# One order table drawn anew, first scores split and narrowed, counts' check and taps moved back, values of two groups in whole rows

## The chip, the cores and the metric

The kernel runs on one core of a Trainium2 chip. The metric is the device time of one execution in microseconds (us); less is better. Three executions of the kernel before took 346.62, 346.76 and 347.51 us, median 346.76. A fourth, profiled one took 346.18 us; the trace and all rows below are of that one.

## What is computed

Three stages follow each other on a batch of 2 sequences of 768 positions: banded attention (each query sees the 96 positions up to itself and the first 8 positions of the sequence), then a gated feed-forward with a convolution of three taps along the sequence, then a gated unit that mixes positions with a 768x768 matrix.

```python
def _attn_ref(q, k, v, n_global, n_local):
    scores = scale * np.matmul(q, k.transpose(0, 1, 3, 2))
    keep = is_global | is_local
    bias = -slopes[:, None, None] * dist[None, :, :]
    scores = np.where(keep, scores + bias, -1e9)
    a = np.exp(scores - np.max(scores, axis=-1, keepdims=True))
    a = a / (np.sum(a, axis=-1, keepdims=True) + 1e-09)
    return np.matmul(a, v)
...
def _moe_ref(x, w_in, conv_w, w_out):
    h = np.maximum(x @ w_in, 0.0)
    hp = np.concatenate([zeros, h, zeros], axis=1)
    for k in range(K):
        conv_out += conv_w[k][None, None, :] * hp[:, k:k + S, :]
    gate = 1.0 / (1.0 + np.exp(-conv_out))
    return (h * gate) @ w_out
...
def _moe2_ref(x, w_in, w_spatial, b_spatial, w_out):
    h = np.maximum(x @ w_in, 0.0)
    u, v = (h[..., :d_ff // 2], h[..., d_ff // 2:])
    v_n = (v - mu) / np.sqrt(var + 1e-06)
    v_s = np.einsum('ts,bsd->btd', w_spatial, v_n) + b_spatial[None, :, None]
    return (u * v_s) @ w_out
```

## The kernel before

**Pieces.** The attention is cut into 6 groups of 256 queries (3 per sequence; `g` counts them), and each group into 4 pairs of heads. A group and a pair make a unit `u` (24 in all): two tiles of 128 queries (`t` = 0, 1) for two heads. A unit's steps are: its q and k are loaded (`qk_load`, tile `qk`, three buffers); TensorE makes the scores (`scores`, L789: 128 queries against 256 keys for each tile and head, the two heads in the two halves of the rows); VectorE adds the bias and takes the minimum of the negated row (`soften`, L808, tile `sb`); ScalarE takes the exponential (L826); the result is transposed, for groups 0 and 1 (`PLAINS`) on TensorE in fp32 (`turn_p`, L839) and for the others by a transposing DMA; TensorE multiplies it with the values (`weigh`, L894, or L900 to L902 for the other groups); VectorE divides (L906 to L911); TensorE turns the output (L942) into the tile `x`.

In group 0 the first tile of queries has only 160 keys that can matter, and L808 reads 160 columns there, while L789 computes 256 for every tile. Groups 0 to 2 (`NATS`) use one fp32 product (4 matmul instructions to a unit, 8 records in the trace); groups 3 to 5 use three products of split operands (12 instructions).

**Values.** `v_load` loads the values of a group into the one tile `v`. For groups 0 and 1 each pair of heads occupies 130 columns (`VW`): a column of ones, 128 values, a column of ones. The ones are set once by a memset on GpSimd (L732) ahead of the first load, and each load writes the 128 columns between them in pieces of 512 bytes.

**Setup.** At the start the two counts (`n_global`, `n_local`) arrive as words; VectorE casts them (`word`, L567), TensorE spreads them over the partitions (L570), VectorE builds the masks and the first two biases (L573 to L594). `flags` (in `setup_rest`, L625 and L635 to L637) tests the counts against what the banded way can do; the answer is read at the end of the kernel. The taps of the convolution are loaded as `craw` and decoded (L655 to L670).

**Weights.** Weights arrive as 8-byte floats in tiles `raw` (512 KB each) and are decoded on GpSimd (L659), ScalarE (L655) and VectorE (L665, L670) and split in two fp16 halves. The feed-forward's matmuls are L1017 (`inner`) and L1087 (`outer`), the third stage's L1171, L1294, L1382 and L1444.

**What sets the order.** Every step is a task of a planner (`Plan`), and the table `ORDER` names for each step in turn its task number, its engine and, where it opens one, its PSUM bank. The instructions of each engine are then issued in exactly that order. While replaying the table the planner keeps a clock of its own from assumed costs. It uses this clock for one thing that reaches the chip: where TensorE's next step would start later than the one before ends, `emit` fills the gap with matmuls whose result nobody reads (`warm`, L988, on the tile `hl`; called fillers below), as many as this formula gives:

```python
share, each = (0.95, 0.213) if start < COLD_TO else (0.8, 0.107)
for _ in range(int(share * (start - busy) / each)):
    warm()
```

Every DMA of the kernel but one is issued by SyncE (SP) in the table's order; a load whose buffer is still in use holds those behind it.

## Time and profile before

| what | value |
|---|---|
| median of three executions | 346.76 us (346.62 to 347.51) |
| the profiled execution | 346.18 us |
| its span, first to last instruction | 344.4 us |
| TensorE busy | 336.9 us (98%) |
| VectorE, ScalarE, GpSimd busy | 305.3, 244.0, 140.6 us |
| moved by DMA | 43.62 MB |

The span is 1.8 us shorter than the profiled execution. A busy TensorE is not a TensorE at work on the result: the fillers count as busy. So the profile has to be read by stretches, and in the first 60 us by what each matmul is.

### The profile page before, as it was taken

The numbers are of one execution on the slowest core, as the hardware profiler recorded it, in microseconds if no ns is written. First come the engines' busy times: TensorE is split into PE (matmuls) and PEld (weight loads), VectorE is DVE, ScalarE is ACT, GpSimd is POOL, SyncE is SP. The second block draws the span as 40 slices with busy tenths as digits, with TensorE's granted clock in tenths as the row PEclk, the third lists the DMA queues.
The fourth block names the chain that finished last, engine by engine and source line by source line (L and its number), as shares of the span: only waits on it lengthen the run. The fifth ranks groups of instructions, "written<-read, shape, count | busy, mean of one in ns | idle before, by whom it ended". The sixth has DMA issues, their size and how long they took to land.

```text
span 344.4 us, 7937 instructions
## 1 busy us (share of the span) xinstructions
PE 336.9 (98%) x2824; PEld 246.5 (72%) x2824; DVE 305.3 (89%) x892; ACT 244.0 (71%) x619; POOL 140.6 (41%) x233
## 2 busy tenths in 40 slices
PE   8999999999999999999999999999999999999993
PEld 5888779898888888888996757755556666654451
DVE  6999999999999999999988899999998999999400
ACT  4999999999999999999865552776555233334331
POOL 5747698599757877737451000000124012010000
PEclk9999999999999999999999999999999999999998
DMA  7999638799659984645770000001461000000332
GB/s 246 349 386 300 214 105 302 175 209 256 125 149 205 278 173 79 184 79 109 102 221 0 2 1 0 2 1 48 126 206 52 0 2 0 3 30 0 124 124 101
DMA packets 46115, 43.62 MB, mean 127 GB/s; under 512 B 34674, under 2 KB 36466, under 8 KB 45554
## 3 DMA queue, kind: packets, MB, share of 16 engines
q1 hardware_dynamic: 46064, 43.02, 45.7%
q8 instruction: 24, 0.39, 0.5%
q14 instruction: 25, 0.20, 0.2%
q10 hardware_dynamic: 2, 0.00, 0.0%
HBM read 31.48 MB, written 3.15 MB: 101 GB/s over the span
## 4 chain that ended last, share of the span: by engine, by line
PE 96%; DMA 1%; DVE 0%; ACT 0%; issue 0%; DVEq 0%
PE bank L1017 19%; PE bank L1087 18%; PE bank L1294 12%; PE bank L1444 9%; PE bank L1382 9%; PE bank L1171 9%; PE bank L789 7%; PE bank L894 4%; PE bank L839 2%; PE bank L988 2%; PE bank L942 2%; DMA qk_dt_float<-in_qk 1%; PE bank L900 1%; PE bank L901 1%; PE bank L902 1%; ACT wk_dt_float L454 0%
## 5 line engine op out<-in xcount | busy, mean ns | idle before, releaser
L1017 PE MATMUL bank<-x_dt_float,w1h_dt_float 128*128 128x260 f16 (+1 forms) x384 | 65.5, 273 | 0.0
L1087 PE MATMUL bank<-hh_dt_float,w2h_dt_float 128*128 128x256 f16 (+2 forms) x192 | 52.4, 273 | 0.0
L1017 PE MATMUL bank<-x_dt_float,w1l_dt_float 128*128 128x260 f16 (+1 forms) x192 | 52.4, 273 | 0.0
L1087 PE MATMUL bank<-hl_dt_float,w2h_dt_float 128*128 128x256 f16 (+2 forms) x192 | 52.3, 272 | 0.0
L1087 PE MATMUL bank<-hh_dt_float,w2l_dt_float 128*128 128x256 f16 (+2 forms) x192 | 52.3, 272 | 0.0
L1030 DVE SCALAR_TENSOR_TENSOR bank<-hp_dt_float,cwt,bank 128x254 f32<-128x254 f32 (+2 forms) x96 | 46.1, 486 | 3.3 <-ACT bank L1024 0.6
L470 POOL TENSOR_TENSOR ph_dt_float<-sb_dt_float,ph_dt_float 128x512 f16<-128x512 f32 x29 | 34.2, 1184 | 20.5 <-ACT ph_dt_float L456 12.4
L1017 PEld LDWEIGHTS <-w1h_dt_float 128*128 128x128 f16 x384 | 37.1, 97 | 5.7
L1087 PEld LDWEIGHTS <-w2h_dt_float 128*128 128x128 f16 x384 | 36.3, 98 | 5.4 <-issue 0.3
L808 DVE CUSTOM_DVE_ANT_0 sb_dt_float<-bank,bias_dt_float 128x256 f32<-128x256 f32 (+1 forms) x96 | 35.4, 402 | 1.6 <-PE bank L789 1.3
L1382 PE MATMUL bank<-ys_dt_float,w3uh_dt_float 128*128 128x384 f16 x128 | 31.2, 326 | 0.0
L826 ACT ACTIVATE sb_dt_float<-sb_dt_float,nb_dt_float 128x256 f32<-128x256 f32 (+1 forms) x64 | 29.6, 491 | 0.0
L659 POOL TENSOR_SCALAR raw_dt_float<-raw_dt_float 128x512 int32<-128x512 uint8 x28 | 19.0, 680 | 24.7 <-DMA raw_dt_float<-in_w 22.0
L1444 PE MATMUL bank<-w4h_dt_float,g_dt_float 128*128 128x512 f16 (+1 forms) x104 | 28.8, 363 | 0.0
L1171 PE MATMUL bank<-w3vh_dt_float,ys_dt_float 128*128 128x512 f16 x96 | 28.5, 379 | 0.0
L470 POOL TENSOR_TENSOR hl_dt_float<-ac_dt_float,hh_dt_float 128x254 f16<-128x254 f32 (+2 forms) x35 | 23.4, 678 | 10.7 <-DVE hh_dt_float L460 8.0
L1444 PEld LDWEIGHTS <-g_dt_float 128*128 128x128 f16 x156 | 15.2, 98 | 15.4
L1171 PEld LDWEIGHTS <-ys_dt_float 128*128 128x128 f16 x144 | 14.1, 98 | 15.3
L1294 PE MATMUL bank<-ws_dt_float,vn_dt_float 128*128 128x384 f16 x144 | 25.0, 326 | 0.0
L1050 ACT ACTIVATE bank<-bank 128x254 f32<-128x254 f32 (+2 forms) x48 | 16.9, 364 | 10.5 <-DVE bank L1030 10.2
L1024 ACT ACTIVATE bank<-hp_dt_float,cwt 128x254 f32<-128x254 f32 (+2 forms) x44 | 21.0, 477 | 0.5
L1055 DVE SCALAR_TENSOR_TENSOR ac_dt_float<-bank,hp_dt_float 128x254 f32<-128x254 f32 (+2 forms) x48 | 19.5, 418 | 2.0 <-ACT bank L1050 1.5
(198 smaller groups left out, 907.6 us busy)
## 6 DMA issues: line engine op xcount, KB each, us to landing
raw_dt_float<-in_w SPq DMA_DIRECT2D x20, 512.0 KB, 6.3
qk_dt_float<-in_qk SPq DMA_DIRECT2D x24, 336.0 KB, 4.6
v_dt_float<-in_vb SPq DMA_DIRECT2D x4, 1024.0 KB, 5.7
out_x<-wk_dt_float SPq DMA_DIRECT2D x11, 256.0 KB, 2.0
raw_dt_float<-in_wst SPq DMA_DIRECT2D x6, 384.0 KB, 3.8
raw_dt_float<-in_w3v SPq DMA_DIRECT2D x4, 512.0 KB, 5.5
raw_dt_float<-in_w3u SPq DMA_DIRECT2D x4, 512.0 KB, 4.4
v_dt_float<-in_vb SPq DMA_DIRECT2D x2, 768.0 KB, 5.1
```

Source lines behind the costliest of these rows:

```text
L470: self.engines[e].tensor_tensor(out=out, in0=in0, in1=in1, op=ALU.subtract)
L789: nc.tensor.matmul(self.ps(sp[h])[:, 256 * t : 256 * (t + 1)], x[r, t * P : (t + 1) * P], y[r, k0[t] : k0[t] + 256], start=n == 0, stop=n ...
L808: nc.vector.tensor_tensor_reduce(out=sb[:, h, :n], in0=self.ps(self.sp[u][h])[:, 256 * t : 256 * t + n], in1=self.m("bias", 2 * p + h)[:, ...
L826: nc.scalar.activation(out=sb[:, h, :n], in_=sb[:, h, :n], func=AF.Exp, scale=-1.0, bias=nb[:, h : h + 1])
L1017: nc.tensor.matmul(self.ps(acc)[:, :nx], w[f][:, k * P : (k + 1) * P], x[:, k, x0:], start=k == n == 0, stop=k == 3 and n == 2,)
L1024: nc.scalar.activation(out=ac(), in_=near(1), func=AF.Copy, scale=tap(1))
L1030: nc.vector.scalar_tensor_tensor(out=ac(), in0=near(j), scalar=tap(j), in1=ac(), op0=ALU.mult, op1=ALU.add)
L1087: nc.tensor.matmul(ps(), w[2 * d + k // 4][:, k % 4 * P : (k % 4 + 1) * P], x, start=k == n == 0, stop=k == 7 and n == 2,)
L1171: nc.tensor.matmul(ps(), x[:, y, k, tk], w[k], start=n == 0, stop=n == 11)
L1294: self.nc.tensor.matmul(self.ps(acc)[:, :HS], v[:, k, x, ek], w[:, k, y], start=n == 0, stop=n == 8)
L1382: nc.tensor.matmul(ps(), w[e4][:, k * P : (k + 1) * P], x[:, y, k, s], start=n == 0, stop=n == 11)
L1444: nc.tensor.matmul(ps(), x[:, y, k, tk], w[k][:, at], start=n == 0, stop=n == 11)
```

## The change

**Scores.** In group 0 the first tile's scores are computed for 160 columns instead of 256 (units 0 to 3, 8 matmuls in all). For units 0 and 1 (`SINGLE`) the two tiles become two steps of the plan, so that VectorE's L808 of the first tile waits for the first two matmuls of the unit alone.

**Counts and taps.** The test of the counts gets a begin of 60 in the planner's time, and the taps' load one of 3.0.

**Values.** For groups 0 and 1 the host lays out an array `vp` in which every pair of heads has its 130 columns, so that a load writes whole rows (6,240 bytes for group 0, 8,320 for group 1). The memset of ones now follows each of these loads, since the load overwrites the columns.

**Planner.** It assumes the first transfer at 2.6 instead of 3.2 and the counts' word at 2.62 instead of 3.1. The table `ORDER` is another from its first line to its last. The program has 65 fillers instead of 60, and as many other matmuls as before.

The diff, of the table one line:

```diff
@@ -47,6 +47,8 @@
 
 BIASES = 2
 
+SINGLE = 2
+
 
 
 HALF = dict(w=8, x=9, h=12, y=12, g=12, v=8, s=16)
@@ -112,61 +114,61 @@
 SIGNS = "ABCDEFGHIJKLMNOPQRSTUVWXYZabcdefghijklmnopqrstuvwxyz0123456789-_"
 
 ORDER = (
-    "CHSAAGAWSDnGAnSAXGABDACGAZSADDAuSAbGAgSAEDBHGCMDAFPAGDCJA0CIGAHDAaP12AJDAKAASAAIDAMAAoGAdDBaSApA3AyDAYSANGAcDAOA",
...
+    "DqGAWSACGAoSAAGAZSA6SAcGABDAvSAEDADDAFPAXSAhSAGDAHDAaP01AMAAIDAbPAKAAJDAqA2AdDApGAeDAQAA0DBdSA5PANGAOAA1DA4P34Ag",
...
 )
 
 
@@ -179,7 +181,7 @@
     ENGINES = ("PE", "DVE", "ACT", "POOL", "SP")
     AFTER = dict(PE=0.21, DVE=0.13, ACT=0.14, POOL=0.1, SP=0.03)
     ISSUE, FLIGHT, LANDING, RATE = 0.45, 0.7, 0.9, 0.41e6
-    BEGIN, FIRST, TURN = 0.75, 3.2, 2.0
+    BEGIN, FIRST, TURN = 0.75, 2.6, 2.0
 
     def __init__(self, tc, room):
         self.tc, self.room = tc, room
@@ -333,9 +335,9 @@
 
 
 class Kernel:
-    def __init__(self, ctx, tc, vb, qk, qf, kf, vf, nw, w1, cw, w2, w3u, w3v, wst, bsp, w4, out):
+    def __init__(self, ctx, tc, vb, vp, qk, qf, kf, vf, nw, w1, cw, w2, w3u, w3v, wst, bsp, w4, out):
         self.tc, self.nc = tc, tc.nc
-        self.vb, self.qk, self.qf, self.kf, self.vf = vb, qk, qf, kf, vf
+        self.vb, self.vp, self.qk, self.qf, self.kf, self.vf = vb, vp, qk, qf, kf, vf
         self.nw, self.w1, self.cw, self.w2 = nw, w1, cw, w2
         self.w3u, self.w3v, self.wst, self.bsp, self.w4, self.out = w3u, w3v, wst, bsp, w4, out
         nc = tc.nc
@@ -508,11 +510,11 @@
 
         self.plan.add(dict(DVE=6.0), judge, reads=[acc, ("flag", 0)], writes=[("junk", 0)])
 
-    def load(self, out, in_, writes, size, reads=()):
+    def load(self, out, in_, writes, size, reads=(), begin=0.0):
 
         self.plan.add(
             dict(SP=Plan.ISSUE), lambda e: self.nc.sync.dma_start(out=out, in_=in_), reads=reads, writes=writes,
-            load=0.05 + size / Plan.RATE,
+            load=0.05 + size / Plan.RATE, begin=begin,
         )
 
     def parts(self, n, hi, lo, src, reads, wh, wl, scale=1.0):
@@ -585,7 +587,7 @@
             nc.vector.tensor_copy(out=rel[:, 256:288], in_=nl.to_broadcast([P, G]))
 
         add(dict(DVE=0.55), far, reads=[("rel", 0)], writes=[("keep", 0)], both=True)
-        add(dict(DVE=0.17), word, writes=[("word", 0)], begin=3.1)
+        add(dict(DVE=0.17), word, writes=[("word", 0)], begin=2.62)
         add(dict(PE=0.25), spread, reads=[("word", 0)], writes=[("words", 1)])
         add(dict(DVE=0.15), words, reads=[("words", 1)], writes=[("words", 0)])
         add(dict(DVE=1.1), masks, reads=[("words", 0)], writes=[("rel", 0), ("keep", 0)], both=True)
@@ -613,7 +615,7 @@
 
         self.load(
             self.craw.rearrange("p n t -> p (n t)").bitcast(I64), self.cw.rearrange("p f j -> p (f j)"),
-            [("craw", 0)], 24576,
+            [("craw", 0)], 24576, begin=3.0,
         )
         self.decode(self.cwt.rearrange("p f j -> p (f j)"), self.craw, [("craw", 0)], [("cwt", 0)])
 
@@ -626,7 +628,7 @@
                     out=self.within[:1, j : j + 1], in0=x[:1], scalar1=at, scalar2=None, op0=op
                 )
 
-        add(dict(DVE=1.0), flags, reads=[("word", 0)], writes=[("flag", 0)], both=True)
+        add(dict(DVE=1.0), flags, reads=[("word", 0)], writes=[("flag", 0)], both=True, begin=60.0)
 
     def counts(self, n):
         nc = self.nc
@@ -715,13 +717,10 @@
         b, c = divmod(g, NCH)
         n = 3 if c == 0 else 4
         if g in PLAINS:
-            v = self.m("v").rearrange("p (n d) -> p n d", d=VW)
-            if g == 0:
-                self.ones_beside(v, ("v", g, "one"))
-            self.load(
-                v[:, : n * NPAIR, 1 : 1 + 2 * D], self.vb[b, c, :, :n].rearrange("p a (n d) -> p (a n) d", d=2 * D),
-                [("v", g, "v")], n * P * 2048, [("v", g, "one")],
-            )
+            size = n * NPAIR * VW
+            v = self.m("v")[:, :size]
+            self.load(v, self.vp[g, :, :size], [("v", g)], 4 * P * size)
+            self.ones_beside(v.rearrange("p (n d) -> p n d", d=VW), ("v", g, "one"))
             return
         v = self.m("v")[:, :2048].rearrange("p (a n) -> p a n", a=4)[:, :n]
         self.load(v, self.vb[b, c, :, :n], [("v", g)], n * P * 2048)
@@ -780,18 +779,27 @@
             pairs = [(hi, hi), (lo, hi), (hi, lo)]
             cost, reads = 0.96, [("qk", u), ("qh", u)]
         sp = self.sp[u] = [self.plan.next("ps") for _ in range(2)]
-
-        def products(e):
-            for t in range(2):
+        short = i == 0 and g in NATS
+        less = 0.16 if short else 0.0
+
+        def products(ts):
+            for t in ts:
                 for n, (x, y) in enumerate(pairs):
                     for h in range(2):
-                        r = slice(64 * h, 64 * h + 64)
+                        r, cols = slice(64 * h, 64 * h + 64), 160 if short and t == 0 else 256
                         nc.tensor.matmul(
-                            self.ps(sp[h])[:, 256 * t : 256 * (t + 1)], x[r, t * P : (t + 1) * P],
-                            y[r, k0[t] : k0[t] + 256], start=n == 0, stop=n == len(pairs) - 1,
+                            self.ps(sp[h])[:, 256 * t : 256 * t + cols], x[r, t * P : (t + 1) * P],
+                            y[r, k0[t] : k0[t] + cols], start=n == 0, stop=n == len(pairs) - 1,
                         )
 
-        self.plan.add(dict(PE=cost), products, reads=reads, writes=sp, half=True)
+        if u >= SINGLE:
+            self.plan.add(dict(PE=cost - less), lambda e: products(range(2)), reads=reads, writes=sp, half=True)
+            return
+        for t in range(2):
+            self.plan.add(
+                dict(PE=0.5 * (cost + 0.283) - less * (t == 0)), lambda e, t=t: products([t]), reads=reads,
+                writes=[(*x, t) for x in sp], half=True,
+            )
 
     def soften(self, s):
         nc, add = self.nc, self.plan.add
@@ -810,7 +818,7 @@
                     scale=-0.125, scalar=3.0e38, op0=ALU.add, op1=ALU.min, accum_out=nm[:, h : h + 1],
                 )
             add(
-                dict(DVE=0.08 + 0.00105 * n), lowest, reads=[self.sp[u][h], ("bias", 2 * p + h)],
+                dict(DVE=0.08 + 0.00105 * n), lowest, reads=[(*self.sp[u][h], t), ("bias", 2 * p + h)],
                 writes=[("sb", s, h), ("nm", s, h)],
             )
         if g in PLAINS:
@@ -1687,10 +1695,12 @@
         near = [np.concatenate([vt[:, k - BACK : k], vt[:, :G]], axis=1) for k in (lo, lo + P) if k]
         rows += (near + near)[:2]
     vb = np.stack(rows, axis=1).reshape(B, NCH, 4, P, DM).transpose(0, 1, 3, 2, 4)
+    vp = vb.reshape(B * NCH, P, 4, NPAIR, 2 * D)[: len(PLAINS)]
+    vp = np.concatenate([vp[..., :1], vp, vp[..., -1:]], axis=-1).reshape(len(PLAINS), P, -1)
     vfull = vt.reshape(B, NT, P, DM).transpose(0, 2, 1, 3)
     w3 = moe2_w_in
     arrays = dict(
-        vb=vb, qk=qk, qf=qt, kf=kt, vf=vfull,
+        vb=vb, vp=vp, qk=qk, qf=qt, kf=kt, vf=vfull,
         nw=np.stack([np.asarray(n_global), np.asarray(n_local)]).astype(np.int64).view(np.uint16),
         w1=moe_w_in.reshape(4, P, 8, P).transpose(1, 2, 0, 3).reshape(P, 8, 512),
         cw=moe_conv_w.reshape(3, 8, P).transpose(2, 1, 0),
```

**TensorE, around the scores of unit 1.** Names: `qk` and `sb` with numbers are buffers, `ident` is the identity of a transposition. Lines L790, L847 and L996 of the changed kernel are L789, L839 and L988 of the one before. Before:

```order
L988 MATMUL bank<-hl_dt_float_76 128x256
L789 MATMUL bank<-qk_dt_float_122 128x256 x4
L839 MATMUL bank<-ident,sb_dt_float_123 128x128 x4
L789 MATMUL bank<-qk_dt_float_130 128x256 x4
L839 MATMUL bank<-ident,sb_dt_float_132 128x128 x4
L839 MATMUL bank<-ident,sb_dt_float_139 128x128 x4
L789 MATMUL bank<-qk_dt_float_88 128x256 x4
L839 MATMUL bank<-ident,sb_dt_float_123 128x128 x4
```

In the changed kernel, the same place:

```order
L996 MATMUL bank<-hl_dt_float_76 128x256
L790 MATMUL bank<-qk_dt_float_122 128x256 x2
L790 MATMUL bank<-qk_dt_float_122 128x160 x2
L847 MATMUL bank<-ident,sb_dt_float_123 128x128 x4
L996 LDWEIGHTS hl_dt_float_76
L996 MATMUL bank<-hl_dt_float_76 128x256
L847 MATMUL bank<-ident,sb_dt_float_132 128x128 x4
L790 MATMUL bank<-qk_dt_float_130 128x160 x2
L790 MATMUL bank<-qk_dt_float_130 128x256 x2
L847 MATMUL bank<-ident,sb_dt_float_139 128x128 x4
```

The two pieces of a unit stand next to each other, one of them is narrower, and a filler has come between two transpositions.

**TensorE, a unit of groups 3 to 5.** Before, each of the 12 stands between other matmuls, as here behind the products with the values:

```order
L902 MATMUL bank<-vh_dt_float_149,pt_dt_float_144 128x65
L789 MATMUL bank<-qh_dt_float32r 128x256 x2
L789 MATMUL bank<-qh_dt_float32r,qk_dt_float32r 128x256 x2
L789 MATMUL bank<-qk_dt_float32r,qh_dt_float32r 128x256 x2
L789 MATMUL bank<-qh_dt_float32r 128x256 x2
L789 MATMUL bank<-qh_dt_float32r,qk_dt_float32r 128x256 x2
L789 MATMUL bank<-qk_dt_float32r,qh_dt_float32r 128x256 x2
L1017 LDWEIGHTS w1h_dt_float_94
```

In the changed kernel, the end of the first of two places where the scores of two units follow each other:

```order
L790 MATMUL bank<-qh_dt_float32r,qk_dt_float32r 128x256 x2
L790 MATMUL bank<-qk_dt_float32r,qh_dt_float32r 128x256 x2
L790 MATMUL bank<-qh_dt_float32r 128x256 x2
L790 MATMUL bank<-qh_dt_float32r,qk_dt_float32r 128x256 x2
L790 MATMUL bank<-qk_dt_float32r,qh_dt_float32r 128x256 x2
L790 MATMUL bank<-qh_dt_float32r 128x256 x2
L790 MATMUL bank<-qh_dt_float32r,qk_dt_float32r 128x256 x2
L790 MATMUL bank<-qk_dt_float32r,qh_dt_float32r 128x256 x2
L1025 LDWEIGHTS w1h_dt_float_92
```

At these two places the second unit of a pair no longer stands between matmuls of another kind.

**GpSimd, the ones beside the values.** `v_dt_float_89` is the tile `v`; L661 is L659 before, L472 is L470, L731 is L732. Before, the one memset stands at the start:

```order
L549 IOTA keep_dt_float_80 128x32
L1039 MEMSET hp_dt_float_178 128x1
L732 MEMSET v_dt_float_89 128x16x2
masks.py:197 MEMSET ident 128x128
masks.py:199 AFFINE_SELECT ident<-ident 128x128
```

In the changed kernel, the second of two, with what stands ahead of it and behind it:

```order
L472 TENSOR_TENSOR w1l_dt_float_100<-wk_dt_float_136,w1h_dt_float_92 128x512
L661 TENSOR_SCALAR raw_dt_float_128<-raw_dt_float_128 128x512
L472 TENSOR_TENSOR w1l_dt_float_101<-wk_dt_float_138,w1h_dt_float_93 128x512
L472 TENSOR_TENSOR w1l_dt_float_102<-wk_dt_float_127,w1h_dt_float_94 128x512
L731 MEMSET v_dt_float_89 128x16x2
L661 TENSOR_SCALAR raw_dt_float_143<-raw_dt_float_143 128x512
L661 TENSOR_SCALAR raw_dt_float_137<-raw_dt_float_137 128x512
```

The memset now waits for a transfer, and the decoding of weights on GpSimd waits behind it.

## Rows read from the trace of the kernel before

**Rows 1.** The page: span; TensorE's busy tenths in 40 slices.

```profile
span 344.4 us, 7937 instructions
PE   8999999999999999999999999999999999999993
```

**Rows 2.** Windows: from:to, length, busy time (count) per engine, clock, DMA.

```profile
0.00:8.40 8.40, 6.96 (x33) 4.37 (x33) 5.47 (x29) 3.48 (x7) 4.58 (x21) 1.00 0.71 251
8.40:60.00 51.60, 51.25 (x431) 43.05 (x430) 49.39 (x164) 50.72 (x122) 37.15 (x58) 1.00 0.80 274
60.00:338.00 278.00, 278.00 (x2360) 198.97 (x2360) 250.44 (x703) 189.23 (x490) 98.85 (x156) 1.00 0.40 96
```

**Rows 3.** Windows of the fillers (L988) alone: TensorE, its weight loads, clock, DMA.

```profile
0.00:8.40 8.40, 4.49 (x23) 2.68 (x23) 1.00 0.71 251
8.40:60.00 51.60, 5.95 (x38) 3.47 (x37) 1.00 0.80 274
```

**Rows 4.** Timeline of the start: start, length, engine, line, operation, count, idle before.

```profile
1.19 2.10 PE L988 MATMUL bank<-hl_dt_float 128*128 128x256 f16 x9 [1.19 <-DVE hl_dt_float L538]
1.19 0.42 SPq L514 DMA_DIRECT2D qk_dt_float<-in_qk  x1
...
2.61 0.15 DVE L567 CAST word<-wt 1x8 f32<-1x8 uint16 x1
...
2.87 0.52 DVE L637 SCALAR_TENSOR_TENSOR cnt<-cnt,word 1x2 f32<-1x2 f32 x3
...
3.22 0.59 PE L570 MATMUL bank<-word,ones 1*128 1x8 f32 x2
...
4.07 1.44 PE L988 MATMUL bank<-hl_dt_float 128*128 128x256 f16 x6 [0.26 <-DVE wf L573]
...
5.42 0.83 DVE L594 SCALAR_TENSOR_TENSOR bias_dt_float<-rel_dt_float,keep_dt_float 128x288 f32<-128x288 f32 x2
...
5.43 2.08 PE L789 MATMUL bank<-qk_dt_float 64*128 64x256 f32 x8
...
7.44 1.05 PE L988 MATMUL bank<-hl_dt_float 128*128 128x256 f16 x8
...
7.56 0.33 DVE L808 CUSTOM_DVE_ANT_0 sb_dt_float<-bank,bias_dt_float 128x160 f32<-128x160 f32 x1 [1.31 <-PE bank L789]
...
8.42 1.13 PE L789 MATMUL bank<-qk_dt_float 64*128 64x256 f32 x8
...
9.49 0.66 PE L839 MATMUL bank<-ident,sb_dt_float 128*128 128x128 f32 x4
```

**Rows 5.** Timeline of TensorE, one unit of groups 3 to 5.

```profile
76.65 0.19 PE L902 MATMUL bank<-vh_dt_float,pt_dt_float 128*128 128x65 f16 x1
76.77 0.39 PE L789 MATMUL bank<-qh_dt_float32r 64*128 64x256 f32 x2
77.00 0.28 PE L789 MATMUL bank<-qh_dt_float32r,qk_dt_float32r 64*128 64x256 f32 x2
...
77.47 0.28 PE L789 MATMUL bank<-qk_dt_float32r,qh_dt_float32r 64*128 64x256 f32 x2
77.68 0.40 PE L1017 MATMUL bank<-x_dt_float,w1h_dt_float 128*128 128x260 f16 x2
```

**Rows 6.** Timeline of TensorE: values' products of unit 3, then of unit 4.

```profile
23.18 1.90 PE L894 MATMUL bank<-v_dt_float,pt_dt_float 128*128 128x65 f32 x16
...
33.12 1.11 PE L894 MATMUL bank<-v_dt_float,pt_dt_float 128*128 128x65 f32 x8
```

**Rows 7.** Timeline of SP: the load of group 1's values.

```profile
25.11 0.68 SPq L514 DMA_DIRECT2D v_dt_float<-in_vb  x1
```

**Rows 8.** Tile `v`: issue to landing of its loads, and its memset.

```profile
L732 POOL MEMSET v_dt_float<- x1: 142/142/142, 1.4 to 1.4; 128x32 f32 x1
...
DMA to landing us min/median/max: 5.0/5.5/6.5
```

**Rows 9.** Line L514, every load and store: issue to landing.

```profile
DMA to landing us min/median/max: 1.8/4.6/8.4
```

More of the change, by code (lines that the diff above doesn't have):

```diff
@@ new lines @@
+    "AArDALGAfACQSA2ABMDAyP5BBSD4GA7GAsDA3ABWSA8A6BLDARGBIP0BgDBOABkP12BhDBKGBNAAPGAzDBjABeP3BiAA9DBJABzP4AYGB3DB2DAU",
+    "AB6P0CUDCsGB5AB0DASAAjA5AiGA-DAtAB1GAkDAVGCXP24B8SB4ABPSCTDBfAATGAlDCRP6CVAEASCWADkP13CuDCKSCtDCSADDDDjSBCGDEDCv",
+    "ABsSCqP6CwAB7DEKGAuGBDA5BlSDBP2D0DEhSDFACxP4DzDDGABXGEFDCrAEEDBEDD1AB9GBYA3CYP0CyDDbP1EGACZABZDAmACaDD2AAnGBaDDH",
+    "P6DCADZP4DIDEHAECP0DcDCLGDaAEIP32BQGEDABFDBbADJDDdP4CDSCbAESP0EVDBcGCjSBRA1EUDDhP6EkDDeAElDCMA5BmGA_ADfDBSDEXAFN",
+    "GBAGEoP24EWAAwSDiDETABtGEmACNDBTDDlP6EiP0EnACODDmDBGACcSFaDFMSBuA3BHGDnDE-DBUAD3P5BvDEjABVGE9DB-A1FbDE7P0BnA6BwD",
@@ new lines @@
+    "DpP2D5AB_DE8ABoDFAAAxGCkGFBP3FdACADCEGD6ABpDDrADLSClA4D7DCzSFeP01DKAF5SE_AFCDC6SBxAFYP6CBAFvDByGEJP3FwDFZACmDDsA",
+    "CdGF8DBqADtDFzP0D8ABrGCFA6CnDFcADMGELAD9DDuAFtP4F9DFxACoDGAP51D-ACGDCpGDgAFyADvDCHDFuAF6P2EZGD_GF-AF0DFgP4DSSF_A",
+    "CCGFhAGMDGJP6F7AGLDEpP0GbDEMAFfGGNGGaDGKACIDGOAFiDGcGEqGGfP21GPAENDGdAErAGYDEyP6CeA5HbSGwDGZGEOAGWSGvDEsACfDGQP4",
+    "DoAGxGEPDC7GGeAG9DDwAG-DC0GGsACgDE0AEzGG0P2CJGGzAGRDC1A3EtDG_GDNA1DTGGBP5E1AC2DEBSEYP4ChAEQDEuADODERGGCAGyAC3DCi",
+    "GEaAHcAE2DHBADxGG1DEbAGtGG7AGDDHCP32HAAEvDE3ADPDG8GEwAHNAFkP5EcDITSC4AHOGGuSHRDDUA1HQDFDP0DQAHpDFlGC5GHqDEdADVDF",
@@ L170 @@
+    "DclAcqDblAcHDc2P3b7AcpDc5DcCAcmDcrP1cIAcyDcOAcNDc6DcUAcuP6b6DcsDc_DdqP7ctDcgDcBDcvDcZDdXP1caDdrAc7DcbAanDdsSaoDc",
+    "hAdwP6c1Dc8DcnAdMDdNDawDa9Dd2P7a-DdADdBDdODdCDdRP2d3Ac9Ad4SdFP7dSDdTDc0DdUAdeP0dEAdYDdlDdtP2dmDdnDdPDdoDdVDc3Ddz",
+    "P4duAdGDdxAdfDdySdgDdvSdZDdHDd-P5dIDdJDdDDdaDdbDeBP3dcDd_AdhDd0AeASdiDdKAd1SdQAeEP2d5P6eFAdWAeGSddAdjAeCAeQP0d6D",
+    "dpAd7Sd8P7eHP1eRDd9DeSSeDSeNP5eKP4eOAeIAePSeJSeLAeMS",
 )
```

94 lines of the change are left out of this document (40 added, 54 removed).

## Prediction

> **What bounds the kernel now.** I read the page first: TensorE's row is full from the second slice to the end of a span of 344.4 us [rows 1]. So the next view splits it. From 60 to 338 us TensorE is busy 278.00 of 278.00 us, and nothing that another engine does sooner can be seen there [rows 2]. In 8.4 to 60 us it is busy 51.25 of 51.60, but 5.95 us of that are 38 fillers (37 start in it), and before 8.4 us fillers make 4.49 us more [rows 3]. Fillers stand where the plan expects TensorE to wait, so some 10.4 us of fillers, 1.2 us ahead of the first one and the 0.35 us of idle time are all that a new order can win, besides making the work itself smaller. In 8.4 to 60 us ScalarE is busy 50.72 and VectorE 49.39 of 51.60 us [rows 2]: these two make the softmax and decode the weights there, and the fillers are what TensorE does meanwhile.
>
> The timeline of the start shows the chain: nine fillers, the spread of the counts at 3.22, six fillers, unit 0's scores at 5.43, eight fillers, unit 1's scores at 8.42 [rows 4]. VectorE has its two biases at 6.25 (5.42 and 0.83 on) and then stands 1.31 us until unit 0's scores end [rows 4].
>
> The granted clock reads 1.00 in all three stretches [rows 2], so its level at the start has to be taken from durations. Fillers of 256 columns follow each other at 0.226 us (1.19 to 3.22 in nine, 4.07 to 5.43 in six) until 7.44 and at 0.11 after it (7.44 to 8.42 in eight, less 0.1 for the change of kind that follows): 1.2 and 2.4 GHz. Before the rise TensorE had worked from 1.19 us on, with gaps of under 0.3 us [rows 4].
>
> A filler is an instruction, not a wait: it runs whether or not its wait would have come. TensorE's work in the new order can therefore be added up, and the end cannot come before it.
>
> **The change part by part, against the profiled execution (346.18 us, span 344.4; the median of the three others is 346.76, so I add the difference to the median).**
>
> *Start.* The order of the changed kernel has seven and five fillers where nine and six were, three fewer at 0.226 us: 0.68 us, and unit 0's scores could start at 4.75. The counts' word allows it: it is cast at 2.61 to 2.76 [rows 4], and the spread would start at 2.77. Removing the counts' test from VectorE's queue (0.52 us at 2.87 for its longest part, [rows 4]) gives nothing by itself, since VectorE waits for TensorE behind it; where it goes, after 60 us, VectorE has 27.6 us free [rows 2], so it costs nothing, and without that room about 0.9 us. The taps' load leaves the first place on SP, which brings unit 0's q and k (issued at 1.19, [rows 4]) forward by one issue, 0.42 us; when they land no row shows. If they land only just ahead of 5.43 now, the scores start at 5.0 and 0.25 us of the gain is lost.
>
> Unit 0 narrowed: a unit takes 1.07 us at full clock (8.42 to 9.49), 0.2 of it for the change of kind before and after, so four passes of 0.22; the first tile has two, and 96 of 256 columns less make 0.16 us, twice that at half clock: 0.32. Its scores then end at 6.44 instead of 7.44. Seven fillers follow instead of eight: if the clock rises where it rose, at 7.44, 4.4 of them run at 0.226 and 2.6 at 0.11, and unit 1 starts at 7.83 instead of 8.42: **-0.6 us**. This is the term that depends on the clock. If the rise came with the work, one us sooner, all seven fillers would run at 0.11, unit 1 would start at 7.3, and the term would be -1.1. The trace has one rise and cannot say which; I take -0.6, the smaller.
>
> The Trainium skill, page "TensorE: Matmul & The Clock Gate", Part 1, says that the warm-up is a budget of time and not a number of matmuls, and that the same kernel shows different numbers of slow matmuls from run to run. By that the term is -0.6 on average; this trace agrees with it in having one rise, and does not test it.
>
> *Narrower scores of units 1 to 3:* three times 0.16, **-0.5**. The pieces of units 0 and 1 stand next to each other in the order, so splitting adds no change of kind. What splitting is to give, an earlier first L808, is hidden: VectorE's biases end at about 5.8 when all shifts by 0.45 (the spread from 3.22 to 2.77), after the first piece, and the transpositions wait behind unit 1 anyway.
>
> *Units next to each other.* In groups 3 to 5 two pairs of units now adjoin. A unit takes 0.91 us to the next kind's start (76.77 to 77.68), its inner passes 0.117 each (77.00 to 77.47 in four), six make 0.70; the second of a pair saves 0.21 and what its lead-in costs, at most 0.09 [rows 5]. 0.25 each: **-0.5**.
>
> *Fillers after the start.* Counted in the order: 46 behind the first three runs of them, where 37 were, the longest run 18, ahead of unit 10. Nine more at 0.11: **+1.0**.
>
> *Whole rows of values.* The 512-byte pieces become rows; the loads move 1.6% more bytes. The trace has no such rows from this array. Loads of `v` take 5.0 to 6.5 us from issue to landing, the six of them with and without pieces [rows 8], so I put the load itself at nought, within 1.5 us for one load. What does change is a wait: the memset of ones (0.14 us, at 1.4 us and behind nothing before, [rows 8]) now follows each of the two loads on GpSimd, with weights' decoding queued behind it, and TensorE's products wait for the memset too. For group 0 the load is now sixth on SP, ahead of the load that needs unit 0's buffer, and I see room. For group 1 it is tight: the load may start when unit 3's products are through, 1.93 us after their start (23.18 to 25.11, [rows 6, 7]). Unit 4's products started 9.94 us after unit 3's [rows 6]. In the new order there lie between them unit 3's products themselves (1.83), a unit's scores (1.07), eight fillers (0.9), 24 feed-forward matmuls (2.6) and three groups of turns (1.2): 7.6 us. Load and memset are ready 1.93 + 5.0 to 6.5 + 0.14 and two handovers of some 0.1, that is 7.3 to 8.8 us after. TensorE waits between -0.3 and 1.2 us; I take 0.4, and of it 0.3 in place of later idle time (0.35 us in that stretch, [rows 2]): **+0.1**.
>
> *All else.* What the new order joins or parts among other groups, and what the other engines do with it, no row prices. From 60 us on not a tenth of a us is idle before [rows 2], so there is nothing to win and something to lose; early on it can go either way by the size of the idle time there, 0.35. I take nought.
>
> Sum: -0.6 - 0.5 - 0.5 + 1.0 + 0.1 = -0.5, rounded with the bounds in mind (the lower end of the start term is -1.1, its upper -0.4) to -0.6. That is 345.6 for an execution like the profiled one and **346.2** for the median. From these terms alone it lies between 345.3 and 347.1.
>
> **Rivals.**
>
> *The start is won in full.* The clock rises with the work and not at its old place: -1.1 instead of -0.6, and with VectorE and ScalarE ahead by as much the 0.35 us of idle time goes too: 346.76 - 1.4 = **345.3**. For it: before 60 us two other engines are as full as TensorE, so their head start counts. Against it: nine fillers more say that the plan sees more waiting, not less.
>
> *Values land late, and the ones behind them.* Slower than before. Group 1's load is queued behind decoded weights' loads; loads of this kernel land up to 8.4 us after issue [rows 9]. Then unit 4's products wait until 1.93 + 8.4 + 0.3 = 10.6 us after unit 3's instead of 7.6: 3.0 us of TensorE, and GpSimd's decoding behind the memset is as late. Less the idle time that it replaces, 346.2 + 2.6 = **348.8**. It decides from a landing 7.3 us after issue on; the longest of the six of this tile is 6.5 [rows 8].
>
> *The start is won and given back.* ScalarE and VectorE work through 8.4 to 60 us without a break; if the new order only lets TensorE run into them earlier, waits appear ahead of its transpositions and the fillers come on top: **346.8**, no change.
>
> **How the numbers follow.** The forecast 346.2 has 0.47, the start in full 0.28, late values 0.13, no gain 0.12. About 0.3% (1.04 us) is what a measurement of this kernel tells from no change: faster means under 345.72, slower over 347.80. Faster: 0.28 and 0.04 of the forecast's edge, 0.32. Slower: 0.13. Within: 0.55. The range 345.0 to 347.9 leaves out the late values and the far end of the full start, 2 in 10.
>
> **What would show it.** Right: unit 1's scores start near 7.8 us; fillers at 0.226 until about 7.4; the score groups of units 1 to 3 take 0.91 us instead of 1.07; fillers after 8 us number 46; TensorE has no idle time after 65 us; in front of unit 4's products (near 32 us) an idle time under 1 us that ends with GpSimd's memset. Wrong: a longer wait there; the rise of the clock elsewhere by more than a us; idle time of TensorE in 60 to 338 us, where VectorE is the next fullest [rows 2]; or waits ahead of the transpositions in 9 to 25 us.

## The result

The changed kernel is slower: 351.06 us, median of six executions (349.97 to 353.93), against 347.14 for six of the kernel before. The ratio is 1.0124, 95% interval [1.0093, 1.0155]. Forecast were 346.2 us and 345.0 to 347.9.

The first profile of it was taken of the slowest of these executions, so a second one was taken of an execution of 350.77 us (the run "again"). Both are read here side by side. The busy times by stretch, first profile (columns: stretch, its length, busy us and instructions of TensorE, its weight loads, VectorE, ScalarE, GpSimd; granted clock, DMA share, GB/s):

```profile
8.40:60.00 51.60, 49.71 (x395) 42.34 (x394) 45.88 (x156) 46.28 (x114) 34.83 (x55) 0.93 0.73 258
60.00:338.00 278.00, 275.22 (x2359) 199.18 (x2357) 253.00 (x701) 194.93 (x500) 107.51 (x166) 1.00 0.40 96
```

and the second, "again":

```profile
8.40:60.00 51.60, 51.36 (x436) 43.83 (x433) 49.65 (x170) 50.17 (x124) 38.17 (x62) 1.00 0.79 274
60.00:338.00 278.00, 274.41 (x2340) 197.24 (x2339) 250.52 (x692) 191.34 (x491) 103.82 (x159) 1.00 0.40 95
```

Where the kernel before had 278.00 of 278.00 us behind 60 us [rows 2], TensorE now lacks 2.78 and 3.59 us. Between 8.4 and 60 us the two profiles differ: 1.89 us idle and a clock of 0.93 in one, 0.24 us idle and full clock in the other. The list of what TensorE waited for, in the first profile (waiting line and releaser; us in total, times, longest):

```profile
PE bank L902 <- POOL v_dt_float L731: 1.8, 1, 1.8
PE bank L908 <- DMA pt_dt_float<-ph_dt_float: 1.8, 1, 1.8
...
PE bank L908 <- DVE ys_dt_float L468: 1.0, 1, 1.0
```

and in "again":

```profile
PE bank L908 <- DMA pt_dt_float<-ph_dt_float: 2.3, 1, 2.3
...
PE bank L908 <- DVE ys_dt_float L468: 1.0, 1, 1.0
...
PE bank L902 <- POOL v_dt_float L731: 0.2, 1, 0.2
```

The two waits of L908 (products of groups 2 to 5) are in both; the one of L902 for group 1's values is an event of single executions. 

> The changed kernel once more, to see which parts of its profile repeat. In the first profile TensorE stood 1.81 us ahead of unit 4's products (33.77, released by the memset of ones behind the values' load, which landed 7.28 us after its issue), ran at the lower clock from there to about 41 us (the sixteen products took 3.36 us instead of 1.9), and stood 0.97 us at 106.99 and 1.80 us at 128.96. That execution took 353.93 us, the five others 349.97 to 352.14. Theory A (the order itself makes the three waits; the clock's fall after the first is what differs between executions): the three waits are here again, at 1.5 to 2.1, 0.8 to 1.1 and 1.6 to 2.0 us, and the time is 350.0 to 350.6 without the fall and 353 to 354 with it. Theory B (the three waits are accidents of that one execution): at least one of them is under 0.3 us.

Neither theory held whole. The wait at group 1's values was 0.17 us, which is the sign that theory B named; the two others came again (1.04 and 2.30 us). So these two belong to the order, and the one at the values does not.

### The profile page after: what moved, and what is told of

The parts are those of the page before. It is cut to its first block, busy times and chain, and to the rows that moved or that the text cites. A ratio compares the mean times of both kernels' runs of the same rounds, so it can differ in the third digit from the quotient of the medians.

```text
span 351.8 us, 7966 instructions
## 1 busy us (share of the span) xinstructions
PE 339.5 (97%) x2829; PEld 249.9 (71%) x2829; DVE 306.3 (87%) x884; ACT 247.5 (70%) x626; POOL 146.3 (42%) x237
## 4 chain that ended last, share of the span: by engine, by line
PE 69%; ACT 17%; DMA 7%; DVE 3%; issue 2%; POOL 0%; ACTq 0%; DVEq 0%; POOLq 0%
PE bank L1302 12%; PE bank L1095 11%; PE bank L1452 9%; PE bank L1390 9%; PE bank L1179 9%; PE bank L1025 8%; DMA pt_dt_float<-ph_dt_float 5%; ACT sb_dt_float L834 4%; PE bank L790 3%; PE bank L902 3%; DMA v_dt_float<-in_vp 2%; ACT ph_dt_float L458 2%; ACT bank L1032 1%; PE bank L847 1%; ACT vh_dt_float L456 1%
## 5 line engine op out<-in xcount | busy, mean ns | idle before, releaser
L472 POOL TENSOR_TENSOR ph_dt_float<-sb_dt_float,ph_dt_float 128x512 f16<-128x512 f32 x31 | 37.2, 1204 | 12.6 <-DVE ph_dt_float L462 6.0
L661 POOL TENSOR_SCALAR raw_dt_float<-raw_dt_float 128x512 int32<-128x512 uint8 x28 | 19.3, 690 | 33.9 <-DMA raw_dt_float<-in_w 27.3
L472 POOL TENSOR_TENSOR hl_dt_float<-ac_dt_float,hh_dt_float 128x254 f16<-128x254 f32 (+2 forms) x35 | 23.5, 676 | 19.7 <-DVE hh_dt_float L462 14.0
L456 ACT ACTIVATE wk_dt_float<-bank 128x512 f32<-128x512 f32 (+1 forms) x11 | 6.0, 575 | 25.2 <-PE bank L1452 21.0
L1058 ACT ACTIVATE bank<-bank 128x254 f32<-128x254 f32 (+2 forms) x48 | 17.7, 369 | 6.5 <-DVE bank L1038 6.4
L1369 ACT ACTIVATE hp_dt_float<-bank 128x260 f32<-128x260 f32 (+1 forms) x47 | 17.8, 385 | 5.5 <-PE bank L1025 5.5
```

What stands on the lines that cost most here:

```text
L472: self.engines[e].tensor_tensor(out=out, in0=in0, in1=in1, op=ALU.subtract)
L661: nc.gpsimd.tensor_scalar(out=lo, in0=top, scalar1=1.0 / 32, scalar2=1.0 / 64 - 0.5, op0=ALU.mult, op1=ALU.add)
L1369: self.nc.scalar.activation(out=out, in_=in_, func=AF.Relu, scale=scale)
```

## The two waits near 102 and 124 us

**The later one: a transposing DMA behind a load.** The sync engine's queue in "again" (timeline; start, us, engine, line, operation):

```profile
114.19 0.33 SPq L516 DMA_DIRECT2D v_dt_float<-in_vb  x1
115.37 7.09 SPq L873 DMA_TRANSPOSE pt_dt_float<-ph_dt_float  x1
```

and in the kernel before, at the same place:

```profile
114.64 2.54 SPq L865 DMA_TRANSPOSE pt_dt_float<-ph_dt_float  x1
117.22 0.70 SPq L514 DMA_DIRECT2D v_dt_float<-in_vb  x1
```

In the old order unit 16's transposing DMA goes first and the 1 MB of group 5's values second; in the new order it is the other way round. Behind the load the issue alone holds the queue 7.09 us instead of 2.54, and unit 16's products wait 2.30 us. The planner lets such a DMA land 4.5 us after its start, or 3.5 us after the loads ahead of it have passed at an assumed rate; in the first profile this one landed 9.9 us after its issue, in "again" 10.4, in the kernel before 5.3. From issue to landing over all transposing DMAs of "again" (tile `pt`), this one being the longest:

```profile
DMA to landing us min/median/max: 4.2/5.0/10.4
```

**The earlier one: two engines in each other's way.** VectorE and GpSimd in "again":

```profile
101.24 1.73 DVE L468 SCALAR_TENSOR_TENSOR vl_dt_float<-v_dt_float,vh_dt_float 128x512 f16<-128x512 f32 x1 [0.45 <-ACT vh_dt_float L456]
102.89 0.41 DVE L468 SCALAR_TENSOR_TENSOR ys_dt_float<-bank,ys_dt_float 128x256 f16<-128x256 f32 x1
```

```profile
100.80 1.61 POOL L472 TENSOR_TENSOR qk_dt_float32r<-qk_dt_float,qh_dt_float32r 128x672 fp32r<-128x672 f32 x1
```

The low half of a quarter of group 4's values (`vl`) takes 1.73 us; the 14 others take 0.68 to 0.75. GpSimd's subtraction of 128x672 elements runs from 100.80 to 102.41, and VectorE ends 0.56 us behind it: it stood until GpSimd was through. Behind `vl` in VectorE's queue is the low half of an output (`ys`), which frees the PSUM bank that unit 13's products wait for. In the kernel before none of the 15 was stretched (longest 0.69 us; columns: minimum, median and maximum of one in ns):

```profile
L466 DVE SCALAR_TENSOR_TENSOR vl_dt_float<-v_dt_float,vh_dt_float x15: 676/682/689, 64.5 to 151.5; 128x512 f16<-128x512 f32 x15
```

The Trainium skill, page "SBUF — State Buffer", section "SBUF: two separate sides", says that VectorE and GpSimd share one pair of ports, that an instruction of VectorE with two inputs in SBUF and one of GpSimd that reads SBUF exclude each other, and that the one that comes second stands for as long as the first runs. The rows above agree: `vl` has two inputs in SBUF, and its end follows GpSimd's.

The edits exchange two neighbours each; all else, the fillers too, is as in the changed kernel:

```diff
 sync engine (turn_first)
+L873 DMA_TRANSPOSE pt<-ph 128x16x128
 L516 DMA v<-in_vb 128x2048
-L873 DMA_TRANSPOSE pt<-ph 128x16x128
 VectorE (ys_first)
+L468 SCALAR_TENSOR_TENSOR ys<-bank,ys 128x256
 L468 SCALAR_TENSOR_TENSOR vl<-v,vh 128x512
-L468 SCALAR_TENSOR_TENSOR ys<-bank,ys 128x256
```

> The changed kernel with two neighbours on the sync engine's queue exchanged: unit 16's transposing DMA is issued ahead of the load of group 5's values (1 MB) instead of behind it. In the profiles so far that DMA landed 9.9 us after its issue in the changed kernel's first profile, and TensorE stood 1.8 to 2.4 us ahead of unit 16's products in all five profiles. Theory C (the 1 MB load ahead of it makes it late): the DMA lands within 6 us, the idle time there is under 0.3 us, and the time is 348.2 to 349.0 instead of 350.8. Rival D (it is queued behind other loads too, or the products wait for something else next): the idle time shrinks to 1 to 2 us and the time is 349.8 to 351.

Measured 348.22 us (347.42 to 349.38; ratio to before 1.0036 [1.0021, 1.0051], before 347.17 in this comparison). The queue now:

```profile
114.82 3.07 SPq L873 DMA_TRANSPOSE pt_dt_float<-ph_dt_float  x1
117.99 0.53 SPq L516 DMA_DIRECT2D v_dt_float<-in_vb  x1
```

The issue takes 3.07 us, the DMA lands 5.7 us after it, and unit 16's products wait for nothing: theory C held. The longest landing of this tile is now 6.4 us:

```profile
DMA to landing us min/median/max: 4.2/4.8/6.4
```

Against the kernel before in each comparison the loss fell from 3.9 to 1.05 us: most of it hung on this one exchange. So it is in all 16 profiles: behind the load the DMA landed 9.9 to 10.5 us after its issue (six profiles), ahead of it 4.6 to 5.7 (ten).

> The changed kernel with two neighbours on VectorE exchanged, near 105 us: the low half of an output of the second matmul (which frees the bank that unit 13's products wait for) comes ahead of the low half of a quarter of group 4's values, which took 1.73 us there instead of the 0.68 us of the 14 others, while GpSimd subtracted 128x672 elements beside it. Theory C: the wait of 0.97 to 1.04 us ahead of unit 13's products goes, and 1.0 us of the time with it: 349.5 to 350.0. Rival D (unit 13's products have another late input, or what is saved is waited for at unit 16's products, since its transposing DMA doesn't come sooner): the wait there grows by as much and the time stays at 350.5 to 351.2.

Measured 349.66 us (348.74 to 351.94, four executions; 1.0093 [1.0057, 1.0129]). The 1.0 us wait went, as theory C has it: `vl` still takes 1.12 us there, but nothing that TensorE needs stands behind it. 0.46 us of small waits, 0.31 of them ahead of the next scores, and 1.78 at unit 16's products stayed.

> Both exchanges: the transposing DMA ahead of group 5's values on the sync engine, and the low half of the output ahead of that of the values on VectorE. Theory C (these two waits are what the new order loses): TensorE's idle time from 100 to 140 us falls from 3.5 us to under 0.5, and the time is 347.2 to 347.8, that of the kernel before, or 346.6 if nothing else becomes late. Rival D: idle time over 1.5 us stays between 100 and 180 us, and the time is 349 or more.

Measured 348.07 us (347.23 to 351.44; 1.0021 [1.0009, 1.0034]); the profiled execution was the slowest of 13, at 351.44, and had the wait at group 1's values again (2.13 us) and one of 1.04 at 23.73 us for decoded weights. From 100 to 140 us TensorE was idle 0.46 us, under the 0.5 of theory C, but the time lies between the theories' ranges. The second exchange shows 0.15 us by the medians (0.5 by the ratios) on top of the first, less than the 1.0 expected and within the scatter.

## Group 1's values

In the first profile of the changed kernel (timeline of all engines):

```profile
26.19 0.33 SPq L516 DMA_DIRECT2D v_dt_float<-in_vp  x1
...
33.58 0.14 POOL L731 MEMSET v_dt_float<- 128x32 f32 x1 [3.00 <-DMA v_dt_float<-in_vp]
...
33.77 3.36 PE L902 MATMUL bank<-v_dt_float,pt_dt_float 128*128 128x65 f32 x16 [1.81 <-POOL v_dt_float L731]
...
37.07 2.08 PE L790 MATMUL bank<-qk_dt_float 64*128 64x256 f32 x8
```

The load was issued at 26.19 and landed at 33.47, 7.28 us later; the memset of ones followed, and unit 4's products waited 1.81 us. Behind that wait TensorE ran at the lower clock, 1.2 GHz:

```profile
30.00:34.00 4.00, 2.19 (x21) 1.78 (x19) 3.96 (x11) 4.00 (x12) 0.92 (x3) 1.00 0.92 281
34.00:38.00 4.00, 4.00 (x20) 3.79 (x21) 1.11 (x4) 1.51 (x4) 2.92 (x4) 0.52 0.91 335
38.00:42.00 4.00, 4.00 (x24) 2.80 (x21) 2.47 (x10) 1.77 (x5) 0.19 (x1) 0.63 0.39 153
```

The sixteen products took 3.36 us. From the start of unit 4's products to that of unit 5's it was 8.24 us here and 5.01 in "again": the fall cost 3.2 us, more than the wait. In `pieces` and `two_moves`, where the clock fell behind this wait too, the same stretch took 6.56 and 6.63 us, a price of 1.6. In the seven profiles in which the load stands at this place the landing took 4.9 to 7.6 us and the wait was 0 to 2.13:

| run | landing, us | wait, us |
|---|---|---|
| ys_first | 4.9 | 0 |
| turn_first | 5.5 | 0 |
| again | 5.6 | 0.17 |
| fill_wait | 5.7 | 0 (filled) |
| pieces | 6.9 | 1.24 |
| after | 7.3 | 1.81 |
| two_moves | 7.6 | 2.13 |

That is the rival "values land late" with its point, 7.3 us, though without the fall of the clock in its price; but what stands ahead of the load is the same in all seven, so it is no yes or no of the change but a share of its executions. In the old order the load landed 6.3 to 6.5 us after its issue in all five profiles, and the products came 8.0 us after it in the first [rows 6, 7].

> The changed kernel, but group 1's values have memory of their own (that of the third stage's weights, free until then), so their load need not wait for unit 3's products; on the sync engine's queue it stands two loads further ahead. All else, the fillers too, as in the changed kernel. The load would be issued near 19 us and land by 27. Theory A (the load's late landing costs the wait and, where the clock falls behind it, some 3.5 us more): no idle time ahead of unit 4's products, granted clock 1.00 in 30 to 40 us, time 348.2 to 348.8, and no execution above 349.5. Rival (the other engines are the limit there, and the 1.8 us come back ahead of the next transpositions): time 350 to 351, with idle time of TensorE over 1 us elsewhere between 34 and 60 us.

```diff
+        m.place(m.at["w3vh"][0], ("v1", 4 * NPAIR * VW, 1))
...
-            v = self.m("v")[:, :size]
+            v = self.m("v1" if g else "v")[:, :size]
```

Measured 350.60 us (348.53 to 352.54; 1.009 [1.0049, 1.013], before 347.24). No wait at the values, though the load, issued at 19.15, landed only at 29.01 and not by 27, but 1.04 and 2.37 us at the two later places. The expected 348.2 to 348.8 was wrong, most likely since the median execution had not waited long there (0.17 us in "again"), and the two later waits were still in place.

> The changed kernel with 17 fillers more, all ahead of unit 4's products: 1.87 us at 0.11, about the wait that stood there. Theory A (the clock falls because TensorE stood still): granted clock 1.00 from 30 to 40 us, the products take 1.9 us instead of 3.36, the values are awaited as long as before, so the time is that of the executions without the fall, 350.0 to 350.7, and none is above 351. Rival (the clock falls by itself at some time in this stretch): granted clock near 0.7 in 30 to 40 us again in the profile, and times that spread from 350 to 354 as before.

```diff
 TensorE, ahead of unit 4's products
+L996 MATMUL bank<-hl 128x256 x17
 L902 MATMUL bank<-v,pt 128x65 x16
```

Measured 350.74 us (350.20 to 352.69). The clock stayed at 1.00 and the products took 1.9 us. That doesn't test theory A: the load landed 5.7 us after its issue here, and in "again", with 5.6 and no fillers, the clock did not fall either. One execution, 352.69, was above the 351 that the theory allowed. Unit 4's products started 1.9 us later than in "again" (34.65 to 32.72; 0.4 of it from a later rise of the clock at the start), and the span was only 0.3 us longer: 0.9 us came back in the later waits (0.42 and 1.99 instead of 1.04 and 2.30).

> The changed kernel, but the values of groups 0 and 1 are loaded as in the kernel before, 128 values of each pair of heads between columns of ones that are set once behind group 0's load; group 1's memset writes to memory that nobody reads. Theory A1 (whole rows with the columns in them are what makes the load slow): it lands 6.5 us or less after its issue at about 26.2, and the idle time ahead of unit 4's products is under 0.8 us; time 349.0 to 349.8. Theory A2 (the load is slow because of the loads around it, and the products come too early in the new order): it lands about 7.2 us after issue as with rows, only the memset's 0.3 us are saved, the idle time is 1.3 to 1.7 us and the time 349.8 to 353.

```diff
-            self.load(v, self.vp[g, :, :size], [("v", g)], 4 * P * size)
+            self.load(
+                v[:, : n * NPAIR, 1 : 1 + 2 * D], self.vb[b, c, :, :n].rearrange("p a (n d) -> p (a n) d", d=2 * D),
```

Measured 352.19 us (350.47 to 353.90, four executions). It landed 6.9 us after issue, inside the range of whole rows, and the time is not lower: nothing here says that the form of the load makes it late, but one landing of one execution can't exclude it.

> Both exchanges, and group 1's values in memory of their own with their load further ahead, as in the run named own_v. Theory C: no wait at group 1's values (0.2 to 1.8 us in four profiles without it) and none at the two other places: median 346.4 to 347.2, with executions that spread by less than 1.5 us, since the wait that differed between executions is gone; faster than the kernel before by 0 to 0.8. Rival D: the spread stays at 2 us or more, and the median is 348 to 349.

It has the two exchanges and the memory of own_v. Measured 347.43 us (346.70 to 348.19, twelve executions; 1.0008 [0.9994, 1.0022], before 347.17), 0.2 above what theory C allowed. Behind the start all waits of over 0.4 us are gone, and with them 3.6 us of the changed kernel's 351.06 and its scatter. It is level with the kernel before, not ahead of it: 0.70 us of small waits stay between 99.97 and 104.18.

## The terms of the sum one by one

**Narrower scores**, in the old order.

```diff
+                        cols = 160 if i == 0 and t == 0 and g in NATS else 256
```

> The kernel before with its own order and its own loads, but the first tile's scores of units 0 to 3 computed for 160 columns instead of 256. Theory by the prediction's terms: 0.16 us for each of units 1 to 3 and 0.16 to 0.32 for unit 0, together 0.64 to 0.80 us less than the kernel before. Rival (behind the start VectorE and ScalarE, 49.4 and 50.7 of 51.6 us busy, set the pace, and what TensorE is sooner comes back as idle time before 60 us): 0 to 0.2 us less.

Measured 346.39 us against 347.12: 0.73 less, 0.9985 [0.9968, 1.0003]. The size fits the terms by the medians; the ratio makes it 0.5 us, and its interval just reaches no change.

**Fillers**, taken out of all_three.

```diff
 TensorE, ahead of unit 10's scores (nine_less)
-L1000 MATMUL bank<-hl 128x256 x18
+L1000 MATMUL bank<-hl 128x256 x9
 behind the start, everywhere (no_fillers)
-L1000 MATMUL bank<-hl 128x256 x46
```

> The kernel of the run all_three with 9 of its 18 fillers ahead of unit 10's scores (near 50 us) taken out: 37 fillers behind the start, as many as the kernel before has. Theory by the prediction's term (a filler is an instruction that costs its 0.11 us whether or not the wait would have come): 0.9 to 1.0 us less than all_three, so 346.4 to 346.6 where the kernel before has 347.2. Rival (the fillers stand for waits of TensorE that are there anyway): as all_three, 347.2 to 347.7, with idle time of 0.5 to 1 us where they were or ahead of the next transpositions.

> The kernel of the run all_three with all 46 fillers behind the start taken out (those of the first 8 us stay). Theory by the prediction's term: up to 46 x 0.11 = 5.0 us less than all_three, 342.4, if no wait takes their place. Rival (the waits for ScalarE and VectorE are there and the fillers filled them): idle time of TensorE of 3 to 5 us between 9 and 64 us, and a time of 346.5 to 347.5; if the granted clock falls in those gaps as it did behind the wait of 1.81 us, 348 to 351.

Measured 348.06 (1.0024 [1.0007, 1.0041]) and 347.87 us (1.0028 [1.0008, 1.0047]): not less than all_three's 347.43, where 1.0 and 5.0 us less were at stake. The stretch of 40 to 60 us without fillers:

```profile
40.00:60.00 20.00, 18.11 (x145) 14.31 (x144) 19.58 (x64) 20.00 (x53) 16.45 (x30) 1.00 0.55 167
```

TensorE stands 1.89 us, and ScalarE is busy 20.00 of 20.00, as it is in all_three. From 8.4 to 140 us TensorE stands 3.2 us here and 0.8 in all_three. In the profile of nine_less it waits 0.62 us for VectorE and 0.98 for a load of q and k that all_three doesn't wait for. So the fillers taken out came back as waits in part, and the reading that fits is that they cost nothing, since ScalarE sets the pace there. Part of no_fillers' time can be the clock's: in three of its twelve executions (348.63 to 349.02 us) its mean was 0.992, in the others 0.995 to 0.999.

**The start.** 

> The kernel before once more, for its profile: in the one profile of it TensorE's clock rose at 7.44 us, while in nine profiles with the changed kernel's start it rose anywhere from 6.87 to about 9.2 us, although the first 6.8 us are the same to 0.02 us in all nine. Theory E (the moment of the rise differs between executions whatever the kernel does): it lies between 6.9 and 9.2 here too, not at 7.44 again, and unit 1's scores start up to 0.6 us later than 8.42. Theory F (it comes with the kernel's own work): 7.4 to 7.5 again.

The fillers ahead of unit 1's scores in that profile and in the two of the changed kernel (before_again, after, again):

```profile
7.45 1.89 PE L988 MATMUL bank<-hl_dt_float 128*128 128x256 f16 x8
9.27 1.51 PE L789 MATMUL bank<-qk_dt_float 64*128 64x256 f32 x8
```

```profile
6.49 1.09 PE L996 MATMUL bank<-hl_dt_float 128*128 128x256 f16 x7
7.51 0.97 PE L790 MATMUL bank<-qk_dt_float 64*128 64x256 f32 x8
```

```profile
6.48 1.68 PE L996 MATMUL bank<-hl_dt_float 128*128 128x256 f16 x7
8.09 0.98 PE L790 MATMUL bank<-qk_dt_float 64*128 64x256 f32 x8
```

In before_again the eight fillers take 1.82 us to the scores, 0.228 each, all at the lower clock; in the profile on which the forecast rests they took 0.98, the clock having risen at 7.44 [rows 4]. In the changed kernel seven fillers take 1.02 us in one execution and 1.61 in the other, though TensorE did the same to 0.02 us until then. The moment of the rise belongs to the execution: among the 16 profiles it lies between about 6.9 us and about 10 (in before_again unit 1's scores still took 1.51 us where [rows 4] has 1.13). The Trainium skill, page "TensorE: Matmul & The Clock Gate", Part 1, expects it to vary from run to run by 0.5 us either way; here it was more (6.9 to 8.1 for the changed kernel in two executions).

```diff
 start of before_start: VectorE
+word<-wt
 keep<-rel
-word<-wt
 sync engine: craw<-in_cw behind qk of unit 1
 fillers: 7, 5, 7 instead of 9, 6, 8
```

> The kernel before with its own order behind the start, but with the start of the changed kernel: 160 columns in the first tile of units 0 to 3, the cast of the counts ahead of the distance masks on VectorE, the test of the counts moved behind 60 us, the taps' load behind unit 1's q and k, and 7, 5 and 7 fillers in the first three runs of them instead of 9, 6 and 8. Theory by the prediction's terms: 0.64 to 0.80 for the narrower scores (0.73 was measured) and 0.7 for three fillers fewer at 0.226, together 1.3 to 1.5 us less than the kernel before: 345.6 to 345.9; the fast start is then what all_three has too, and the 1.5 us that all_three lacks were lost behind 90 us by its order. Rival (a head start ends at ScalarE and VectorE, and the moment at which the clock rises decides more than the fillers): the start gives nothing beyond the narrower scores, 346.3 to 346.7, with idle time before 60 us larger by 0.5 to 0.7.

Measured 348.33 us, slower than before (1.0052 [1.0031, 1.0073]). Neither theory had it, because of where I had put the test of the counts:

```profile
60.95 1.10 DVE L635 CAST cnt<-wt 1x2 f32<-1x2 int16 x1
62.09 0.95 DVE L637 SCALAR_TENSOR_TENSOR cnt<-cnt,word 1x2 f32<-1x2 f32 x3
63.07 0.26 DVE L625 TENSOR_SCALAR within<-cnt 1x1 f32<-1x1 f32 x3
```

```profile
60.88 1.16 POOL L470 TENSOR_TENSOR ph_dt_float<-sb_dt_float,ph_dt_float 128x512 f16<-128x512 f32 x1
```

```profile
PE bank L1088 <- DVE x_dt_float L470: 2.0, 1, 2.0
```

Its seven small instructions take 2.3 us there (the first cast 1.10, 0.15 at the start), beside GpSimd's subtractions (the first cast ends at 62.05, GpSimd's instruction at 62.04), and VectorE has other work queued behind them.

> As the run before_start, but the test of the counts stands behind VectorE's last work for the third stage, near 322 us, where VectorE is idle. In before_start it stood at 60.95 us, took VectorE 2.3 us there, and TensorE waited 2.03 us behind it. Theory by the prediction's terms (the start's gain reaches the end): that wait goes, and 1.3 to 1.5 us less than the kernel before are left, 345.5 to 345.7; less than before_narrow by 0.6 to 0.7. Rival (the three fillers fewer give nothing, since ScalarE and VectorE follow the start at their own pace): the wait goes, and the time is that of before_narrow, 0.5 to 0.9 less than the kernel before, with more idle time before 60 us.

Measured 346.54 us (ratio 0.9985 [0.9971, 0.9999], before 347.08). The wait is gone, and the time is that of the narrower scores alone: three fillers fewer show no further gain. The two intervals together leave about 0.8 us either way, so a gain of the forecast size is not excluded. This kernel is the one that beats both: by 4.5 us the changed kernel, by 0.54 the kernel before, with an interval that just excludes no change; before_narrow has the same ratio.

## Why the prediction was wrong

- **"All else: I take nought"** is the step that failed. It held that nothing could be seen behind 60 us and took the middle of an unknown; the profile said that there was only something to lose there, and TensorE stood 3.3 us ("again"; 2.8 in the first profile) at two places where one instruction stood ahead of a neighbour that TensorE awaited sooner. Exchanging both took 3.0 of the 3.9 us away (two_moves), the transposing DMA alone 2.9. I counted TensorE's rows and did not look at what stood ahead of each transposing DMA on the sync engine.
- **Fillers, +1.0**: wrong by its whole size as far as nine_less shows. "The end cannot come before it" is true of TensorE's sum, but it is a bound and not the pace: ScalarE was busy 50.72 of 51.60 us [rows 2], and removing 46 fillers gained nothing.
- **Start, -0.6**: the rows came as forecast (unit 1 at 7.51 and 8.09, between and beyond the two cases), but no gain of it showed at the end in the old order, with about 0.8 us of scatter either way. That the test of the counts costs nothing behind 60 us, because VectorE has 27.6 us free there, holds for its place in the changed kernel (near 70 us, the cast 0.15 us) and not for every place: at 60.95 us in before_start TensorE waited 2.03 us behind it. The base was off as well: the one profile of before had an early rise, and took 346.18 where the median of 29 executions was 347.2.
- **Narrower scores, -0.5 and the share of unit 0**: in keeping with what was measured, 0.73 us by the medians for all four units, though not clear of no change.
- **Adjoining pairs, -0.25 each**: the rows bear it out. Two units take 1.62 us to the next kind's start, where one alone takes 0.91 [rows 5], 0.20 saved; it did not matter for the end.

```profile
87.60 0.39 PE L790 MATMUL bank<-qh_dt_float32r 64*128 64x256 f32 x2
...
89.01 0.28 PE L790 MATMUL bank<-qk_dt_float32r,qh_dt_float32r 64*128 64x256 f32 x2
89.22 0.40 PE L1025 MATMUL bank<-x_dt_float,w1h_dt_float 128*128 128x260 f16 x2
```

- **Values, +0.1**: the mechanism was right and the spread mis-sized: "within 1.5 us for one load" was 2.7 us from the shortest to the longest in seven profiles, and the fall of the clock behind the wait was not in the price at all. Of the whole loss it is the smaller part: 0.64 us of the median (two_moves to all_three), within the scatter.
- **The bounds of the sum**: the lower one, 345.3, doesn't follow "from these terms alone". With the start at -1.1 they sum to -1.0, which is 345.8; the rest is the idle time of 0.35 us that only the first rival counts in.
- **What would show it**: "idle time of TensorE in 60 to 338 us" was named as what would make it wrong, and that is what came.

## What to carry to other kernels

A stretch without idle time on the full engine means that a new order alone, with the same work, can only lose there; go through its queues for each long transfer or shared resource that moved ahead of something awaited, instead of pricing the rest at nought. Fillers placed by a plan stand for waits: price them by the engine that is awaited, not by their own length. Free time of an engine in a long stretch says nothing of one place in it. TensorE may go on at half its clock behind a wait: in the first profile 1.8 us of waiting cost 5.
